# Dilated q in residue order, row sums in two parts, and a static instruction order from measured durations, in an attention and soft-MoE kernel

## The chip, the cores and the metric

The kernel runs on one core of a Trainium2 chip. The metric is the device time of one execution in microseconds (us). Within a profile, times count from the start of the span; the reported time is 1.7 to 1.8 us longer than the span. A ratio is the mean time of one kernel's fast runs over the mean of the other's fast runs of the same rounds, so it is not quite the ratio of the medians quoted beside it.

The engines: PE does matmuls, PEld its weight loads, ACT evicts and exponentiates, DVE transposes and multiplies, POOL issues the loads, SP issues the stores. The 16 DMA engines move the data. The granted clock is the share of PE's full clock that the profile shows as let through. Labels such as L731 are lines of that kernel's kernel.py; L1 and L2 alone are the two layers of the experts.

## The reference

Sliding-window attention (8 batches, 8 heads, 576 tokens, head size 64) and then a soft mixture of experts over all 4608 tokens. Cut to what matters:

```python
mask_plain = (rel >= 0) & (rel < 32)                                  # heads 0..3
mask_dil = (rel >= 0) & (rel < 128) & (rel % 4 == 0)                  # heads 4..7
attn = softmax(where(mask, q @ k.T / 8, -1e9)); x = concat_heads(attn @ v)   # (4608, 512)

logits = x @ phi                                      # 8 experts x 4 slots = 32 columns
d = softmax(logits, over tokens)
slot_input = d.T @ x                                  # needs ALL tokens
slot_out[e] = relu(slot_input[e] @ w1[e]) @ w2[e]     # needs all of w1 and w2
out = softmax(logits, over slots) @ slot_out          # (4608, 512) f32, 9.44 MB
```

No output row exists before the attention of every token is done, and none before every expert's w2 has been used. The inputs are 28 MB of q, k, v and 34 MB of weights.

## The kernel before

Attention works in 16 halves, a plain and a dilated one for each batch. Each operation is registered with a guessed duration and a priority; a small list scheduler simulates the five engines and the DMA queue and fixes one static order for each engine. On the chip each engine then runs its list strictly in order, waiting on semaphores. A wrong guess does no harm to the result; it can only put an operation at a bad place in a list.

```python
PE_SLOW = 1.5
LAT = 0.07                          # from the end of an op to where others see it
def pet(n, cols): return n * max(cols / 2.4, 30.0) * PE_SLOW / 1000.0
...
if o.kind == "dma":                 # the scheduler's model of a load
    qfree = max(qfree, o.end + 1.3) + o.bytes / 422e3
    o.vis = qfree + 1.5
```

q, k and v are turned by DVE in 32x32 blocks so that the head dimension lies on the partitions. In the dilated half a query block is every fourth token. A token's bf16 pair takes 4 bytes, so a step of four tokens is 8 elements, 16 bytes:

```python
dve.transpose(au(o_dst, [[1, 18], [18, 32]]), au(o_stg + ..., [[32, 18], [1, 32]]))   # q, k and v
...
pe.matmul(pf(h, 128 * rr, [[1, 128]]),                  # L477: 4 heads run side by side
          a(ok + 2 * res + par, [[8, 128]], 32 * h, 32),   # k: weights, 16-byte step
          a(oq + 2 * res + par, [[8, 128]], 32 * h, 32))   # q: moving, 16-byte step
pe.matmul(pf(h, 256, [[1, 64]]),                        # L484: the 64 left-over queries
          a(ok + 2 * (320 + 128 * r) + par, [[2, 128]], 32 * h, 32),
          a(oq + 1024 + par, [[2, 64]], 32 * h, 32))
```

The first layer (L1) and the transposes of its result are followed by 36 row-sum matmuls and the second layer (L2). L2 is cut into column halves s = 0 and 1, and into expert groups; the w2 of experts 6 and 7 is loaded last, as four column-half "slabs". So the first half of the columns can be finished, multiplied out and stored while the second-half slabs are still on their way. NA = 3 row groups of 512 rows are stored in halves, the other six whole.

```python
wq += [w2_slab(6, 0), w2_slab(7, 0), w2_slab(6, 1), w2_slab(7, 1)]      # the last loads
...
for es_ in ((0, 1, 2, 3), (4, 5), (6, 7)):
    for s in range(2):
        l2(es_, s)                                  # "L260" = experts 6,7, half 0; "L261" half 1
...
for G in range(NA):                                 # 12 first-half output tiles
    for j in range(4): out_tile(G, j, 0, 256, ...)  # PE matmul, then ACT or DVE evicts
    store(G, 0, 256, ...)
```

The softmax here doesn't subtract the row's maximum and nothing guards it: scores larger than these inputs give would overflow.

## Time and profile before

| | before |
|---|---|
| time, median of 4 | 186.97 us (186.74 to 187.33) |
| span | 185.3 us |
| last slot-input sum (end of attention) starts on PE | 140.2 us |
| L2 | 150.5 to 156.95 us |
| first store issued | 158.3 us |
| from the first store to the end of the span | 27 us |

The page's rows by 40 slices of 4.63 us, for the kernel before: a digit is the busy share in tenths, PEclk the granted clock, GB/s what the DMA engines wrote (loads turn f32 into bf16 on the way, so 211 GB/s written is 422 GB/s read).

```profile
PEclk9999999999999999999999979999965799999755
DMA  5999999999999999999999999999999990599996
GB/s 69 203 211 209 210 211 211 211 210 212 211 210 211 211 210 211 210 211 211 209 211 211 211 211 217 213 213 213 217 211 200 198 160 12 183 348 398 425 416 274
```

The load stream never stops until about 152 us. Then DMA is almost idle for a slice and a half, and then it stores to the end.

Groups of instructions by line and shape, for the kernel before. The columns after the bar are total busy us, the mean ns of one, and the idle time before them with what ended it.

```profile
L450 DVE STREAM_TRANSPOSE ar<-ar 128x576 uint32<-128x576 uint32 x48 | 57.5, 1245 | 9.1 <-DMA ar<-in_v_dram 3.4 <-PE ps L521 2.9 <-PE ps L484 1.7
L477 PE MATMUL ps<-ar 32*128 32x128 bf16 x256 | 18.2, 413 | 0.0
L477 PEld LDWEIGHTS ps<-ar 32*128 32x128 bf16 x256 | 8.3, 146 | 7.0 <-issue 5.0
L484 PE MATMUL ps<-ar 32*128 32x64 bf16 x128 | 4.1, 200 | 0.0
```

The timeline of PE and the store queue in the tail, for the kernel before: start, length, engine, line, count, and in brackets the wait before it. L685 is the last slot-input sum, L731 is L1, L765 the row sums, L781 is L2, L812 the output tiles.

```profile
140.20 0.75 PE L685 MATMUL ps<-ar 96*128 96x32 bf16 x22 [0.65 <-ACT ar L673]
141.84 4.82 PE L731 MATMUL ps<-ar 128*32 128x512 bf16 x48 [0.90 <-DVE ar L719]
148.22 1.36 PE L765 MATMUL ps<-ar 128*128 128x1 bf16 x36
150.48 6.47 PE L781 MATMUL ps<-ar 128*32 128x256 bf16 x128 [0.36 <-DVE ar L754]
156.88 3.37 PE L812 MATMUL ps<-ar 128*128 128x256 bf16 x18
158.29 14.50 SPq L831 DMA_DIRECT2D out_dram<-ar  x12
```

All 128 L2 matmuls run through in one block, with no wait for a weight: the last slab had landed before L2 came to it. The output tiles of both halves come after all of L2.

### The profile page before, as it was taken

The numbers are of one execution on the slowest core, as the hardware profiler recorded it, in microseconds if no ns is written. First come the engines' busy times: TensorE is split into PE (matmuls) and PEld (weight loads), VectorE is DVE, ScalarE is ACT, GpSimd is POOL, SyncE is SP. The second block draws the span as 40 slices with busy tenths as digits, with TensorE's granted clock in tenths as the row PEclk, the third lists the DMA queues.
The fourth block names the chain that finished last, engine by engine and source line by source line (L and its number), as shares of the span: only waits on it lengthen the run. The fifth ranks groups of instructions, "written<-read, shape, count | busy, mean of one in ns | idle before, by whom it ended". The sixth has DMA issues, their size and how long they took to land.

```text
span 185.3 us, 5336 instructions
## 1 busy us (share of the span) xinstructions
PE 132.0 (71%) x2268; PEld 90.2 (49%) x2268; DVE 113.9 (61%) x186; ACT 105.2 (57%) x167; POOL 51.5 (28%) x97
## 2 busy tenths in 40 slices
PE   0027897788797988798898699888566989984000
PEld 0014555567566657467567476656434477321000
DVE  6897277688997968697498596433601010997000
ACT  0008467776869779479769846957541411995000
POOL 7679813413424332323850000270000000000000
PEclk9999999999999999999999979999965799999755
DMA  5999999999999999999999999999999990599996
GB/s 69 203 211 209 210 211 211 211 210 212 211 210 211 211 210 211 210 211 211 209 211 211 211 211 217 213 213 213 217 211 200 198 160 12 183 348 398 425 416 274
DMA packets 21735, 40.78 MB, mean 220 GB/s; under 512 B 2000, under 2 KB 9168, under 8 KB 20944
## 3 DMA queue, kind: packets, MB, share of 16 engines
q0 software_dynamic: 17152, 30.94, 90.3%
q1 hardware_dynamic: 4560, 9.50, 13.5%
q8 instruction: 18, 0.29, 0.6%
q14 instruction: 5, 0.04, 0.1%
HBM read 61.93 MB, written 9.44 MB: 385 GB/s over the span
## 4 chain that ended last, share of the span: by engine, by line
PE 41%; ACT 17%; DVE 16%; DMA 12%; issue 5%; ACTq 0%; DVEq 0%; POOLq 0%
DMA ar<-in_v_dram 12%; ACT ar L499 9%; PE ps L460 7%; PE ps L477 7%; PE ps L812 5%; DVE ar L450 4%; DVE ar L565 4%; PE ps L781 3%; PE ps L554 3%; PE ps L731 3%; ACT ar L527 3%; PE ps L521 2%; ACT ar L621 2%; PE ps L644 2%; PE ps L467 2%
## 5 line engine op out<-in xcount | busy, mean ns | idle before, releaser
L450 DVE STREAM_TRANSPOSE ar<-ar 128x576 uint32<-128x576 uint32 x48 | 57.5, 1245 | 9.1 <-DMA ar<-in_v_dram 3.4
L499 ACT ACTIVATE ar<-ps 128x1152 bf16<-128x1152 f32 (+1 forms) x32 | 37.9, 1185 | 26.9 <-PE ps L484 22.7
L460 PE MATMUL ps<-ar 128*128 128x320 bf16 (+1 forms) x128 | 24.4, 318 | 18.6 <-DVE ar L450 12.5
L565 DVE TENSOR_TENSOR ar<-ps,fs 96x768 bf16<-96x768 f32 (+1 forms) x32 | 26.3, 823 | 1.3
L527 ACT ACTIVATE ar<-ps 128x768 bf16<-128x768 bf16 x32 | 24.8, 829 | 3.0 <-PE ps L521 2.9
L460 PEld LDWEIGHTS ps<-ar 128*128 128x128 bf16 x128 | 11.2, 103 | 23.2 <-DVE ar L450 13.8
L521 PE MATMUL ps<-ar 128*128 128x128 bf16 x192 | 17.3, 234 | 2.9 <-ACT ar L652 1.8
L554 PE MATMUL ps<-ar 128*128 128x65 bf16 x320 | 15.3, 199 | 5.0 <-ACT ar L499 2.3
L477 PE MATMUL ps<-ar 32*128 32x128 bf16 x256 | 18.2, 413 | 0.0
L561 DVE RECIPROCAL fs<-ps 96x12 f32<-96x12 f32 (+1 forms) x32 | 6.3, 196 | 17.8 <-PE ps L554 17.6
L824 DVE TENSOR_SCALAR ar<-ps,fs 128x256 f32<-128x256 f32 (+1 forms) x24 | 12.8, 609 | 7.0 <-PE ps L812 7.0
L554 PEld LDWEIGHTS ps<-ar 128*128 128x128 bf16 x320 | 12.6, 101 | 7.7 <-ACT ar L499 3.2
L521 PEld LDWEIGHTS ps<-ar 128*128 128x128 bf16 x192 | 13.1, 120 | 4.4 <-PE ps L554 1.9
L327 POOL DMA_DIRECT2D ar<-in_k_dram x16 | 9.3, 581 | 18.5 <-DVE ar L450 12.8
L327 POOL DMA_DIRECT2D ar<-in_v_dram x16 | 8.8, 551 | 17.3 <-DVE ar L450 6.8
L344 POOL DMA_DIRECT2D ar<-in_moe_w_dram x12 | 6.4, 584 | 24.1 <-DVE fs L693 24.1
L821 ACT ACTIVATE ar<-ps,fs 128x256 f32<-128x256 f32 (+1 forms) x24 | 12.2, 584 | 0.1
L812 PE MATMUL ps<-ar 128*128 128x256 bf16 (+1 forms) x48 | 11.2, 333 | 1.3 <-DVE ar L824 0.6
L337 POOL DMA_DIRECT2D ar<-in_moe_w_dram x16 | 11.7, 737 | 0.0
L477 PEld LDWEIGHTS ps<-ar 32*128 32x128 bf16 x256 | 8.3, 146 | 7.0 <-issue 5.0
L327 POOL DMA_DIRECT2D ar<-in_q_dram x16 | 8.8, 548 | 9.7 <-DVE ar L450 4.9
L644 PE MATMUL ps<-ar 128*128 128x288 bf16 x64 | 10.2, 307 | 1.2 <-ACT ar L628 1.2
(64 smaller groups left out, 163.1 us busy)
## 6 DMA issues: line engine op xcount, KB each, us to landing
ar<-in_moe_w_dram POOLq DMA_DIRECT2D x32, 512.0 KB, 24.9
out_dram<-ar SPq DMA_DIRECT2D x6, 1024.0 KB, 10.3
ar<-in_k_dram POOLq DMA_DIRECT2D x16, 288.0 KB, 20.4
ar<-in_q_dram POOLq DMA_DIRECT2D x16, 288.0 KB, 20.7
ar<-in_v_dram POOLq DMA_DIRECT2D x16, 288.0 KB, 20.4
out_dram<-ar SPq DMA_DIRECT2D x6, 512.0 KB, 6.3
fs<-in_moe_phi_dram SPq DMA_DIRECT2D x1, 64.0 KB, 1.9
```

The costliest lines, as they stand in the source:

```text
L327: return pool.dma_start(a(o_stg + (s * 3 + j) * 1152, [[1, 1152]]), src[b, 4 * dl:4 * dl + 4].rearrange("h (p t) d -> (h p) (t d)", p=32))
L450: op(DVE, lambda j=j, o_dst=o_dst: dve.transpose(au(o_dst, [[1, 18], [18, 32]]), au(o_stg + (st * 3 + j) * 1152, [[32, 18], [1, 32]])), 1. ...
L460: pe.matmul(pf(h, 0, [[1, W]]), a(o_id, [[1, 128]]), a(msk, [[1, W]]), start=True, stop=False)
L477: last = pe.matmul(pf(h, 128 * rr, [[1, 128]]), a(ok + 2 * res + par, [[8, 128]], 32 * h, 32), a(oq + 2 * res + par, [[8, 128]], 32 * h, 3 ...
L499: eo = op(ACT, lambda P=P, W=W: act.activation(a(P, [[W, 4], [1, W]]), AP(ps, 0, [[4096, 128], [512, 4], [1, W]]), ACTF.Exp, scale=SCALE), ...
L521: last = pe.transpose(pb(bank.idx, bb * 256 + par * 32, [[64, 4], [1, 32]]), src, a(o_id, [[1, 128]]))
L527: op(ACT, lambda t=t, bank=bank: act.activation(a(o_vb[vs] + 3 * t * VBK, [[66, 12], [2, 32], [1, 2]]), pb(bank.idx, 0, [[64, 12], [1, 32] ...
L554: last = pe.matmul(pf(bank.idx + x, 65 * t, [[1, 65]]), w, a(VB + t * VBK + 66 * h, [[1, 65]]), start=True, stop=True)
L565: op(DVE, lambda hp=hp, bank=bank: dve.tensor_tensor(a(ox + 128 * hp, [[64, 2], [256, NT], [1, 64]], 0, rows), pf(bank.idx, 0, [[512, 2], ...
L644: last = pe.matmul(pf(bank.idx, 0, [[1, 288]]), a(o_phis + 128 * c, [[1, 128]]), a(o_xt[xt] + 576 * c + 288 * g, [[1, 288]]), start=(c == ...
L812: op(PE, lambda: pe.matmul(pf(bank.idx, 0, [[1, cw]]), a(o_et + 512 * G + j, [[4, 128]]), a(o_so + c0, [[1, cw]]), start=True, stop=True), ...
L824: op(DVE, lambda: dve.tensor_scalar(dst, src(), sca, None, op0=AluOp.mult), dvet(cw, True), prio + .1, reads=[bank, b_rinv], writes=wr, na ...
```

## The change

Its intent: read dilated q with a 4-byte step, take most row sums out of the tail, and feed the scheduler durations and latencies measured for each kind of operation. Cut to its core:

```diff
-PE_SLOW = 1.5
+PE_SLOW = 1.1
-    LAT = 0.07
+    LAT = {"PE": 0.24, "ACT": 0.06, "DVE": 0.05, "POOL": 0.06, "SP": 0.06}
-        return n * max(cols / 2.4, 30.0) * PE_SLOW / 1000.0
+        return (40.0 + n * max(cols / 2.4, 27.0)) * PE_SLOW / 1000.0
...     (and new durations in about ten op() calls; the op that turns v on PE now
         also waits for the buffer it is evicted to, a part that no run isolates)
+            for x in range(4):       # dilated q only; else one transpose as before
+                na = (18 - x + 3) // 4
+                t0, t1 = x, 18 + x
+                at = [(t % 4) * 144 + t // 4 for t in (t0, t1)]
+                last = dve.transpose(
+                    au(o_dst + 2 * at[0], [[1, na], [9, 16], [at[1] - at[0], 2]]),
+                    au(src + 64 * x, [[128, na], [1, 32]]))
-                                a(oq + 2 * res + par, [[8, 128]], 32 * h, 32),
+                                a(oq + 288 * res + par, [[2, 128]], 32 * h, 32),
-                            a(oq + 1024 + par, [[2, 64]], 32 * h, 32),
+                            a(oq + 256 + par, [[2, 16], [288, 4]], 32 * h, 32),
...
+        if i == 13:
+            row_sums(0, 7, 15 * PERIOD)      # 28 of the 36 matmuls, inside attention
+    row_sums(7, 9, T1 + 4)                   # the other 8
-    op(PE, rs_fn, pet(36, 30), T1 + 3, ...)  # all 36, between L1 and L2
```

More of the change, by code (lines that the diff above doesn't have):

```diff
@@ L172, in run @@
             free[o.eng] = o.end
-            o.vis = o.end + self.LAT
+            o.vis = o.end + self.LAT[o.eng]
             if o.kind == "dma":
@@ L447, in half, with turn @@
         oq, ok = ok, oq
-        for j, o_dst in ((1, ok), (0, oq), (2, ov)):
-            op(DVE, lambda j=j, o_dst=o_dst: dve.transpose(
-                au(o_dst, [[1, 18], [18, 32]]),
-                au(o_stg + (st * 3 + j) * 1152, [[32, 18], [1, 32]])),
-               1.24, pr("T") + (0.5 if j == 2 else 0.0), reads=[b_stg[st][j]],
-               writes=[b_kqv[kq][j]], name=f"T{i}{'qkv'[j]}")
+        def turn(j, o_dst):
+            src = o_stg + (st * 3 + j) * 1152
+            if not (dl and j == 0):
+                return dve.transpose(au(o_dst, [[1, 18], [18, 32]]), au(src, [[32, 18], [1, 32]]))
+            for x in range(4):
[5 more added lines that the diff above has]
+                    au(src + 64 * x, [[128, na], [1, 32]]))
+            return last
+        for j, o_dst in ((1, ok), (0, oq), (2, ov)):
+            op(DVE, lambda j=j, o_dst=o_dst: turn(j, o_dst),
+               1.43 if dl and j == 0 else 1.24, pr("T") + (0.5 if j == 2 else 0.0),
+               reads=[b_stg[st][j]], writes=[b_kqv[kq][j]], name=f"T{i}{'qkv'[j]}")
         def sc_fn(r):
@@ L494, in half @@
             dr = 1.6 * r
-            op(PE, lambda r=r: sc_fn(r), 0.35 + pet(4, 300) + pet(6, 100), pr("SC") + dr,
+            op(PE, lambda r=r: sc_fn(r), (1.2 if dl else 0.9) * PE_SLOW, pr("SC") + dr,
                reads=[bq, bk, b_id, b_md if dl else b_mp],
@@ L523, in tb_fn @@
                 return last
-            op(PE, tb_fn, pet(6, 128), pr("TB") + 1.0 * t, reads=[bv, b_id], writes=[bank],
+            op(PE, tb_fn, pet(6, 128), pr("TB") + 1.0 * t, reads=[bv, b_id], writes=[bank, b_vb[vs][t]],
                name=f"TB{i}{t}")
@@ L557, in pv_fn @@
                 return last
-            op(PE, pv_fn, pet(2 * NT, 80), pr("PV") + 0.5 * hp, reads=b_vb[vs] + bP, writes=[bank],
+            op(PE, pv_fn, pet(2 * NT, 65), pr("PV") + 0.5 * hp, reads=b_vb[vs] + bP, writes=[bank],
                name=f"PV{i}{hp}")
@@ L582, in pz_fn @@
                 return last
-            op(PE, pz_fn, pet(8, 80), pr("PV") + 1.2, reads=b_vb[vs] + bP, writes=[bank],
+            op(PE, pz_fn, pet(8, 65), pr("PV") + 1.2, reads=b_vb[vs] + bP, writes=[bank],
                name=f"PZ{i}")
@@ L616, in half @@
             n = 6 if not dl else (2 if x else 8)
-            op(PE, xt_fn, pet(n, 110), pr("XT") + 0.4 * x, reads=[bx, b_id], writes=[bank],
+            op(PE, xt_fn, pet(n, 128 if dl else 96), pr("XT") + 0.4 * x, reads=[bx, b_id], writes=[bank],
                name=f"XT{i}{x}")
@@ L671, in half @@
         ek = b % 2
-        op(PE, et_fn, pet(11, 80), pr("ET"), reads=[b_et, b_sel], writes=[bank], name=f"ET{b}")
+        op(PE, et_fn, pet(11, 32), pr("ET"), reads=[b_et, b_sel], writes=[bank], name=f"ET{b}")
         op(ACT, lambda bank=bank: act.activation(
@@ L689, in si_fn @@
             return last
-        op(PE, si_fn, pet(22, 80), pr("SI"), reads=[b_ek[ek], b_xp[xi], b_xd[xi]], writes=[bank],
+        op(PE, si_fn, pet(22, 32), pr("SI"), reads=[b_ek[ek], b_xp[xi], b_xd[xi]], writes=[bank],
            name=f"SI{b}")
@@ L695, in half, with row_sums, fn @@
            dvet(128, True), pr("SA"), reads=[bank], rmw=[b_siacc], name=f"SA{b}")
+    def row_sums(g0, g1, prio):
+        bank = Bank(f"rs{g0}")
+        def fn():
+            last = None
+            for t in range(4 * g0, 4 * g1):
+                last = pe.matmul(pf(bank.idx, t, [[1, 1]]), a(o_et + 512 * (t // 4) + t % 4, [[4, 128]]),
+                                 a(o_rm, [[1, 1]]), start=True, stop=True)
+            return last
+        op(PE, fn, pet(4 * (g1 - g0), 72), prio, reads=[b_et, b_rm], writes=[bank], name=f"RS{g0}")
+        op(DVE, lambda: dve.reciprocal(f(o_rinv + 4 * g0, [[1, 4 * (g1 - g0)]]),
+                                       pf(bank.idx, 4 * g0, [[1, 4 * (g1 - g0)]])),
+           .2, prio + .2, reads=[bank], writes=[b_rinv], name=f"RR{g0}")
     last_ex = [None]
@@ L735, in l1_fn @@
                 return last
-            op(PE, l1_fn, pet(4, 560), T1 + 0.2 + g, reads=[b_sit] + b_w1[4 * g:4 * g + 4],
+            op(PE, l1_fn, pet(4, 900), T1 + 0.2 + g, reads=[b_sit] + b_w1[4 * g:4 * g + 4],
                writes=[bank], name=f"L1{g}{x}")
@@ L757, in bass_dilated_sliding_attn__then__soft_moe_slots_kernel @@
            reads=[bank], writes=[b_htz], name=f"HE{g}")
-    bank = Bank("rs")
-    def rs_fn(bank=bank):
-        last = None
-        for t in range(36):
-            last = pe.matmul(pf(bank.idx, t, [[1, 1]]), a(o_et + 512 * (t // 4) + t % 4, [[4, 128]]),
-                             a(o_rm, [[1, 1]]), start=True, stop=True)
-        return last
-    op(PE, rs_fn, pet(36, 30), T1 + 3, reads=[b_et, b_rm, b_sit], writes=[bank], name="RS")
-    op(DVE, lambda bank=bank: dve.reciprocal(f(o_rinv, [[1, 36]]), pf(bank.idx, 0, [[1, 36]])),
-       .2, T1 + 3.2, reads=[bank], writes=[b_rinv], name="RSr")
     sobank = [Bank("soA"), Bank("soB")]
@@ L785, in fn @@
             return last
-        op(PE, fn, pet(8, 270), T1 + 5 + 2 * es[0] + 20 * s,
+        op(PE, fn, pet(8, 300), T1 + 5 + 2 * es[0] + 20 * s,
            reads=[b_htz] + [b_w2[e][s] for e in es], rmw=[sobank[s]], name=f"L2{es[0]}{s}")
```

## The prediction

> **What bounds the kernel now.**
> 1. Loads: in the 40-slice view DMA is at 9 and moves about 211 GB/s (as written) from 5 us to 148 us; the slice at 153 to 157 us shows 12. So all inputs and weights are in at about 152 us, whatever the engines do.
> 2. Attention is slower than its inputs. In the timeline the same PE piece (a batch's first dilated scores, L460 then L477) stands at 62.2 and 77.2 us: 15.0 us a batch, PE busy 6.1 of every 7 us. A batch's loads with two weight pieces take about 13.3 us (estimate: 5.6 MB read at 2 x 211 GB/s). The last k, q, v land by about 111 us (estimate), but the last scores end at 127.1 and the last slot-input sum at 141.3.
> 3. The tail: L1 from 141.8 (clock granted 0.57), row sums L765 148.2 to 149.6, L2 150.5 to 156.9, first store issued at 158.3. From there to the end is 27 us, of which 9.44 MB at 425 GB/s is 22.
>
> So every us by which the first store comes earlier is a us of time, until the landing of the last weights sets it.
>
> **What the change does.**
> - *q in residue order.* In the dilated scores each group of four heads' matmuls (128 columns) takes (1.14 - 0.41)/3 = 0.24 us; in the plain ones (96 columns, step 4 bytes) (0.44 - 0.20)/5 = 0.05. The Trainium skill ("SBUF — State Buffer", cachelines note) says that accesses crossing a 16-byte line pay a penalty; q's step there is 16 bytes, so the trace agrees. With step 4 a group should take 0.1 (k, still 16 bytes, loads its weights in 141 ns, not 92). The 64 left-over queries get an inner step of 576 bytes: their two groups go from 0.05 to about 0.13. Net about 0.55 us per scores operation, 16 of them: 9 us of PE, nearly all on the critical path.
> - *Four transposes.* 1.245 us becomes about 1.43[...]: +1.5 us on DVE in all, which has room.
> - *Row sums.* 28 of 36 move into attention; 1.36 us between L1 and L2 becomes about 0.3: 1 us.
> - *Order.* Better costs should remove some waits of PE on ACT (5 us at L460 for L499), and let first-half outputs go before second-half L2. Worth 0 to 4 us; can go wrong.
>
> **Sum.** A batch falls from 15.0 to about 13.8 us, near the loads' 13.3. The last slot-input sum comes 8 to 10 us earlier, L2 could start at about 140. Then weights bound it: the first-half slabs of the last two experts land at about 147, first store at about 150, the second half lands at 152. About 8 of the 9 to 11 us gained reach the end. 152 + 22 + about 3 = 177 us span, plus 1.7 us between span and time: **179.5 us**. Range 176.5 to 184. Chances: faster by over 2% 0.86, within 2% 0.12, slower 0.02.
>
> **What would show it.** L477 x16 falls from 1.14 us to about 0.5, MATMUL mean from 413 ns to about 210; L484 rises. Batch period 13.5 to 14. Slot-input sum at 130 to 135. L2's last operations wait for the weight DMA. No slice near 12 GB/s between loads and stores.
>
> **What would make it wrong.** k's strided weight load bounds L477 (gain halved: about 183); the new order stalls PE or puts second-half L2 ahead of first-half outputs (first store at 154: 183); PE idles for loads and is granted less clock in the tail; stores slow the last loads.

## The result, and the profile after

| | before | after | predicted |
|---|---|---|---|
| time, median of 4 | 186.97 us | 184.78 us (183.87 to 184.89) | 179.5 (176.5 to 184) |
| ratio of fast runs | | 0.987 (0.9835 to 0.9906) | 0.96 |
| last slot-input sum starts | 140.2 | 132.5 | 130 to 135 |
| first-half slabs landed, L2 on them starts | (not waited for) | 149.8 | 147 |
| last slab landed | 154.1 | 155.2 | 152 |
| last L2 ends | 156.95 | 157.1 | not given |
| first store issued | 158.3 | 153.0 | 150 |
| span | 185.3 | 183.1 | 177 |

Attention did end 7.7 us earlier, inside the predicted window. The time fell by 2.2 us. The same three rows of the page, for the kernel after:

```profile
PEclk9999996999999999999999999995559995799755
DMA  5999999999999999999999999999999997299997
GB/s 69 201 211 207 211 210 213 211 210 214 208 212 212 208 210 213 209 209 211 211 213 209 212 209 217 212 217 212 214 215 207 197 192 159 71 341 397 408 428 317
```

The load stream looks as it did. The hole in DMA after it has moved by one slice and is narrower, but it is still there (71 GB/s). The groups that answer to those shown of before, for the kernel after:

```profile
L489 PE MATMUL ps<-ar 32*128 32x128 bf16 x256 | 7.8, 239 | 0.0
L489 PEld LDWEIGHTS ps<-ar 32*128 32x128 bf16 x256 | 5.5, 146 | 4.5 <-issue 4.5
L496 PE MATMUL ps<-ar 32*128 32x64 bf16 x128 | 6.3, 274 | 0.0
L458 DVE STREAM_TRANSPOSE ar<-ar 128x160 uint32<-128x160 uint32 x16 | 5.9, 442 | 0.4 <-DMA ar<-in_q_dram 0.4
L458 DVE STREAM_TRANSPOSE ar<-ar 128x128 uint32<-128x128 uint32 x16 | 4.8, 373 | 0.0
```

The dilated matmul fell from 413 to 239 ns, the weight load of k stayed at 146 ns, and the left-over matmul rose from 200 to 274 ns, all as predicted. The tail of the kernel after, on PE and the store queue (L697 is the last slot-input sum, L798 is L2, L829 the output tiles):

```profile
132.50 0.77 PE L697 MATMUL ps<-ar 96*128 96x32 bf16 x22 [0.31 <-ACT ar L685]
142.50 3.67 PE L798 MATMUL ps<-ar 128*32 128x256 bf16 x96 [0.84 <-DVE ar L785]
149.84 1.05 PE L798 MATMUL ps<-ar 128*32 128x256 bf16 x16 [3.67 <-DMA ar<-in_moe_w_dram]
151.37 1.47 PE L829 MATMUL ps<-ar 128*128 128x256 bf16 x6 [0.48 <-ACT ar L811]
155.21 1.89 PE L798 MATMUL ps<-ar 128*32 128x256 bf16 x16 [2.38 <-DMA ar<-in_moe_w_dram]
157.04 2.31 PE L829 MATMUL ps<-ar 128*128 128x256 bf16 x13
152.96 18.24 SPq L848 DMA_DIRECT2D out_dram<-ar  x12
```

This is the whole story in seven lines. L2 of experts 0 to 5 is done at 146.2 and then PE waits 3.7 us for the first-half slabs. Six of the twelve first-half output tiles follow. The list of PE then says "last L2", whose slab lands at 155.2, and the other six tiles, which need nothing more, stand behind it. Only one store is out by then; the second is issued at 158.25, where the first of before was issued at 158.29. And the last L2 takes 1.89 us where the same 16 matmuls took 1.05 at 149.84.

Two-us stretches of the kernel after, with busy us (and count) of each engine and, at the end of a row, the granted clock, DMA share and GB/s:

```profile
core 0: us, PE busy (x) PEld busy (x) DVE busy (x) ACT busy (x) POOL busy (x), PEclk, DMA share, GB/s
153.00:155.00 2.00, 0.00 (x0) 0.00 (x0) 0.36 (x1) 0.14 (x1) 0.00 (x0) 0.50 0.55 148
155.00:157.00 2.00, 1.79 (x16) 1.03 (x16) 0.00 (x0) 0.00 (x0) 0.00 (x0) 0.50 0.42 142
157.00:159.00 2.00, 1.98 (x14) 1.28 (x12) 1.31 (x4) 1.85 (x5) 0.00 (x0) 0.72 0.00 0
```

From 157 to 159 us DMA moves nothing. PE stood idle from 153 to 155 us, and the clock granted to it is 0.50 when the last L2 comes. The Trainium skill ("TensorE: Matmul & The Clock Gate", Part 1) names half clock as the throttled state, and here the 1.89 us against 1.05 us agree. It also says that an idle window of about 3.4 us brings half clock back, and this the trace of after does not bear out. The 16 matmuls right behind a wait of 3.67 us (at 149.84) ran in 1.05 us. The clock fell at 151.3 us, before the wait of 2.38 us began. And it was 0.50 from 124.0 to 137.7 us too (the 5s in the PEclk row), though no wait of PE in the 14 us before was longer than 1.4 us. What makes the clock fall stays open here.

### The profile page after: what moved, and what is told of

The parts are those of the page before. It is cut to its first block, busy times and chain, and to the rows that moved or that the text cites. A ratio compares the mean times of both kernels' runs of the same rounds, so it can differ in the third digit from the quotient of the medians.

```text
span 183.1 us, 5337 instructions
## 1 busy us (share of the span) xinstructions
PE 122.1 (67%) x2268; PEld 86.1 (47%) x2268; DVE 113.5 (62%) x211; ACT 105.3 (58%) x167; POOL 51.5 (28%) x97
## 3 DMA queue, kind: packets, MB, share of 16 engines
q1 hardware_dynamic: 4560, 9.50, 13.7%
## 4 chain that ended last, share of the span: by engine, by line
DMA 49%; DVE 20%; PE 14%; ACT 3%; issue 3%; POOL 2%; POOLq 0%; DVEq 0%; ACTq 0%
DMA ar<-in_moe_w_dram 21%; DMA ar<-in_k_dram 15%; DMA ar<-in_v_dram 14%; DVE ar L452 8%; PE ps L829 3%; DVE ar L577 3%; PE ps L472 3%; DVE ar L841 3%; ACT ar L511 3%; PE ps L566 2%; DVE ar L412 2%; PE ps L533 1%; PE ps L479 1%; DVE ar L417 1%; PE ps L798 1%
## 5 line engine op out<-in xcount | busy, mean ns | idle before, releaser
L452 DVE STREAM_TRANSPOSE ar<-ar 128x576 uint32<-128x576 uint32 x40 | 48.6, 1245 | 6.7 <-DMA ar<-in_k_dram 6.3
L472 PE MATMUL ps<-ar 128*128 128x320 bf16 (+1 forms) x128 | 23.8, 312 | 16.1 <-DVE ar L452 12.5
L539 ACT ACTIVATE ar<-ps 128x768 bf16<-128x768 bf16 x32 | 25.7, 826 | 3.6 <-PE ps L533 3.6
L327 POOL DMA_DIRECT2D ar<-in_v_dram x16 | 8.8, 550 | 13.8 <-DVE ar L452 8.4
L636 ACT ACTIVATE ar<-ps 128x1024 bf16<-128x1024 bf16 x8 | 8.2, 1022 | 7.6 <-PE ps L623 7.6
L829 PE MATMUL ps<-ar 128*128 128x256 bf16 (+1 forms) x48 | 11.5, 362 | 1.4 <-ACT ar L811 0.5
L798 PE MATMUL ps<-ar 128*32 128x256 bf16 x128 | 6.6, 291 | 6.9 <-DMA ar<-in_moe_w_dram 6.0
## 6 DMA issues: line engine op xcount, KB each, us to landing
ar<-in_moe_w_dram POOLq DMA_DIRECT2D x32, 512.0 KB, 27.9
```

The lines of the kernel that those rows point to most:

```text
L327: return pool.dma_start(a(o_stg + (s * 3 + j) * 1152, [[1, 1152]]), src[b, 4 * dl:4 * dl + 4].rearrange("h (p t) d -> (h p) (t d)", p=32))
L452: return dve.transpose(au(o_dst, [[1, 18], [18, 32]]), au(src, [[32, 18], [1, 32]]))
L472: pe.matmul(pf(h, 0, [[1, W]]), a(o_id, [[1, 128]]), a(msk, [[1, W]]), start=True, stop=False)
L539: op(ACT, lambda t=t, bank=bank: act.activation(a(o_vb[vs] + 3 * t * VBK, [[66, 12], [2, 32], [1, 2]]), pb(bank.idx, 0, [[64, 12], [1, 32] ...
L829: op(PE, lambda: pe.matmul(pf(bank.idx, 0, [[1, cw]]), a(o_et + 512 * G + j, [[4, 128]]), a(o_so + c0, [[1, cw]]), start=True, stop=True), ...
```

## The experiments

The theory after reading the two traces (called A): *from about 150 us on, the time is set by when the weight slabs land and by what stands before and behind the last L2 on PE. Attention that ends earlier only waits longer.* Its rivals: the static order made attention faster and q did nothing (B); the time follows attention one for one (C); early stores don't help, or only slow the loads (D).

Twelve kernels ran, four to a chip, with five rounds each. The medians of before on the three chips were 186.7, 187.3 and 187.5 us, so the ratios are the better numbers.

### q alone, in the kernel before

The turn, its four transposes and the two new steps were put into before. No duration was touched, and the order of all engines was confirmed to be that of before.

```diff
+        def turn(j, o_dst): ...                # as in the change
-                a(oq + 2 * res + par, [[8, 128]], 32 * h, 32),
+                a(oq + 288 * res + par, [[2, 128]], 32 * h, 32),
-                a(oq + 1024 + par, [[2, 64]], 32 * h, 32),
+                a(oq + 256 + par, [[2, 16], [288, 4]], 32 * h, 32),
```

> The kernel before with the turned q and its four transposes alone; the instruction order is that of before. Theory A (the end is set by the landing of the last weight slabs at 154 to 155 us; work on PE before that is hidden beyond some 2 us): attention ends 6 to 9 us earlier (last slot-input sum at 132 to 135, not 141.3), but the last L2 waits for the slab and ends at about 155.5, first store at about 157; time 185 to 186. Rival B (the gain of the change comes from its instruction order, q brings little even inside attention): last slot-input sum at 138 or later, time 186.5 to 187. Rival C (time follows attention one for one): 179 to 181.

186.43 us, ratio 0.9983 (0.9956 to 1.0009): nothing that can be told from before. Rival C is out. Between A and B this run does not decide: the last slot-input sum started at 137.4 us, 2.8 us earlier than in before and not the 6 to 9 that A expected, and the time lies just above A's range and just below B's. DVE now waited for the inputs instead:

```profile
DVE ar L452 <- DMA ar<-in_v_dram: 6.4, 4, 4.0
DVE ar L452 <- DMA ar<-in_k_dram: 2.9, 4, 0.9
```

These are two rows of the waits of q_only (total us, times, longest); before has one such row, of 3.4 us. Part of the freed PE time became waiting for q, k, v. The 2.8 us that did arrive at the tail were spent in front of the slab: the first store came at 157.7, 0.6 us earlier than in before.

### Everything but q

```diff
-            if not (dl and j == 0):
+            if True:                           # one transpose, natural order
-                a(oq + 288 * res + par, [[2, 128]], 32 * h, 32),
+                a(oq + 2 * res + par, [[8, 128]], 32 * h, 32),
-                a(oq + 256 + par, [[2, 16], [288, 4]], 32 * h, 32),
+                a(oq + 1024 + par, [[2, 64]], 32 * h, 32),
```

> The kernel after with q in its natural order again (16-byte step, one transpose); instruction order and row sums as in after. Theory A: attention ends 4 to 8 us later than in after (slot-input sum at 137 to 141, not 133.3); L2 then ends at 155 to 157, near the slab's landing, so only 0 to 2 us of that reach the time: 185 to 187. Rival B: below 185.5 and attention nearly as early as in after. Rival C: 190 or more.

184.30 us, ratio 0.9873 (0.9841 to 0.9904), the same as the whole change (0.987). It was slightly faster than theory A expected. So of the change's 1.3%, order and row sums bring all. In this profile they bring it with attention as late as in before (the last slot-input sum started at 140.0 us), which speaks against rival B; but a later run with the same attention program shows 135.9, so how much the order does for attention is not settled. That the time does not come from there is what the next two runs test.

### The last L2 before all first-half tiles

If the gain lies in the place of the last L2, taking that place away must take the gain away, and leave attention as fast as it is.

```diff
+    by = {o.name: o for o in sc.ops}
+    for G in range(3):
+        for j in range(4):
+            by[f"O{G}{j}0"].ord = by["L261"]   # an edge for the scheduler, no semaphore
```

> The kernel after (turned q, split row sums, its order) with one edge: the last second-half L2 stands before all first-half output tiles, as in before. Attention still ends near 133 us. Theory A (what the time gained came from first-half outputs going out before the last slab is worked off, not from attention): first store at 157.5 to 158.5, time 186 to 187, all of the change's gain gone though attention is 8 us earlier. Rival C (attention's gain reaches the time): 184.3 to 185.2, as after.

187.51 us, ratio 1.0014 (0.999 to 1.0038), 0.5 us above the expected range. The whole gain is gone, though the last slot-input sum started at 134.25 us, 6 us earlier than in before. L2 and the first store of l2_first:

```profile
150.31 1.05 PE L798 MATMUL ps<-ar 128*32 128x256 bf16 x16 [2.41 <-DMA ar<-in_moe_w_dram]
155.46 1.89 PE L798 MATMUL ps<-ar 128*32 128x256 bf16 x16 [4.09 <-DMA ar<-in_moe_w_dram]
158.96 6.60 SPq L848 DMA_DIRECT2D out_dram<-ar  x6
```

6 us of earlier attention have become 2.4 us and 4.1 us of waiting for slabs, and a last L2 at half clock. Rival C is refuted.

### Only the place of the last L2, in the kernel before

The mirror image: the old q, the old row sums, the old durations, and two edges.

```diff
+    by["L260"].ord = by["L241"]       # experts 0..5 of both halves first
+    by["L261"].ord = by["O230"]       # all 12 first-half tiles before the last L2
```

> The kernel before with two ordering edges in the tail alone: the last experts' L2 after the other experts' L2, and all first-half output tiles before the last second-half L2. No change to attention, q or row sums. Theory A: first store at about 156.5, no idle DMA after it, time 184 to 185: as fast as the whole change. Rival C: attention still ends at 141, so 186.5 or more.

185.26 us, ratio 0.9887 (0.9858 to 0.9917), just above the expected range: two edges give what the whole change gives (0.987), with the last slot-input sum at 141.0 us. Its tail, by PE and the store queue:

```profile
150.60 4.64 PE L781 MATMUL ps<-ar 128*32 128x256 bf16 x112 [0.32 <-DVE ar L754]
157.13 8.22 SPq L831 DMA_DIRECT2D out_dram<-ar  x7
157.78 1.05 PE L781 MATMUL ps<-ar 128*32 128x256 bf16 x16
```

The last L2 starts 2.6 us later than in after and the time is about the same, because the first-half stores run meanwhile.

### All twelve tiles before the last L2, in the kernel after

```diff
+    by["L261"].ord = by[f"O{NA - 1}30"]
```

> The kernel after with one ordering edge: all twelve first-half output tiles stand before the last experts' second-half L2 on PE, not six. Theory A: the six tiles no longer wait behind the slab landing at 155.2; three first-half stores go out by about 155 and fill the 4 us in which DMA is idle (156 to 160): time 182 to 183, 2 to 2.5 us less than after. Rival D (the store phase starts when the second half is there, whatever came before; early stores only delay the slabs): slabs land 1 us or more later and the time stays at 184.5 to 185.

182.68 us, ratio 0.9786 (0.9755 to 0.9818), which is 0.8% under after's ratio. Rival D is refuted: the last slab had landed at 155.1 us and was used at 155.27, within 0.1 us of after. The tail of outs_first, and its stretches:

```profile
151.71 2.11 PE L829 MATMUL ps<-ar 128*128 128x256 bf16 x12 [0.57 <-ACT ar L811]
155.27 1.05 PE L798 MATMUL ps<-ar 128*32 128x256 bf16 x16 [1.45 <-DMA ar<-in_moe_w_dram]
```

```profile
155.00:157.00 2.00, 1.21 (x17) 0.94 (x18) 0.00 (x0) 0.38 (x1) 0.00 (x0) 0.90 1.02 343
157.00:159.00 2.00, 2.00 (x11) 1.44 (x10) 1.53 (x4) 1.74 (x5) 0.00 (x0) 0.50 0.98 328
```

DMA is busy from 155 to 159 us, where after had 142 GB/s and then none. PE's wait is 1.45 us and not 2.38, and the last L2 runs at full clock (1.05 us).

Why did the scheduler put only six tiles there? Its own simulation answers it. Printed from the order it built for after (simulated end of issue, when the data is seen):

```
w2s_70   seen at 146.29 us     the chip: first-half L2 waits until 149.84
w2s_71   seen at 151.26 us     the chip: 155.2
L261     simulated start 151.26, after tile O110, the sixth
```

The change corrected the durations of the engines and left the model of the loads 3.5 to 4 us early. In the simulation the last slab is there when the sixth tile is done. On the chip it is not, and an in-order engine can't step around it.

### outs_first without q

> outs_first with q in its natural order. Attention ends at about 140.8, L2 of the first half at about 153.8 and not 151.1, so the first store at about 155.6 and not 153.0. Theory A says that what q gains in attention (7.5 us) can reach the time only as far as the first-half slabs' landing at 150 lets it: here up to 2.7 us earlier first store; time 183 to 184.3, 0.5 to 1.5 us over outs_first. If q is worth nothing even then: 182.7 as outs_first.

The edit is that of "everything but q" on top of the edge. 183.19 us, ratio 0.9775 (0.9742 to 0.9807): no slower than outs_first (0.9786). The expected 0.5 to 1.5 us did not appear. In this profile attention's last sum started at 135.9 us, 4 us earlier than in no_q, which has the same attention program, and not at the expected 140.8. The first-half slabs had landed by 148.7 us, and L2 ran through with no wait for them:

```profile
145.16 4.58 PE L798 MATMUL ps<-ar 128*32 128x256 bf16 x112 [0.57 <-PE ps L780]
```

So the case that the expectation was about, L2 late because of attention, did not occur in it. One profile each is a poor measure of the end of attention (see below); the six times of each are not. After against no_q (0.987 and 0.9873) and outs_first against no_q_outs (0.9786 and 0.9775, on two chips) say the same: q in residue order is worth nothing measurable with either tail.

### Whole rows instead of slabs

```diff
-    for e in range(6):
+    for e in range(8):
         wq += [w2_piece(e, 0), w2_piece(e, 4)]
-    wq += [w2_slab(6, 0), w2_slab(7, 0), w2_slab(6, 1), w2_slab(7, 1)]
```

> The kernel after with the last two experts' w2 loaded in whole-row pieces (8 KB runs) instead of column-half slabs (1 KB runs). If the slabs' short runs are why the last weights land at 155.2 and not at the 152 of the prediction: last landing at 152 to 153 us and no slow slices from 142 to 154. If the drain of the queue is why: still 154 to 155. Without the halves the first store comes after both L2, at landing plus about 3.5 us; time 183 to 185.5.

187.91 us, ratio 1.0047 (1.0007 to 1.0086): slower than before, and 2.4 us above the expected range. It was to show whether the short runs of the slabs make the landing late. They don't: L2 waited for the last weights until 155.0 us here too.

```profile
155.00 3.44 PE L797 MATMUL ps<-ar 128*32 128x256 bf16 x32 [5.59 <-DMA ar<-in_moe_w_dram]
```

But the rate did hold up longer, and then tapered off: 209 GB/s at 149 to 150 us, then 147, 98, 45, 16, 8. So the lateness is in the drain of the queue, and the halves are worth keeping: without them the first store came at 159.8 us. One impurity: with the halves gone, all of L2 stands before all the tiles, as in l2_first. The intervals of the two ratios (1.0047 and 1.0014) overlap, so this run shows no loss beyond that of the early tiles.

The trace holds for each load the 16 moments at which the DMA engines reported their part done. The distance from the first to the last of the 16:

```
                         after    before
a load near 50 us        2.0      1.9  us
a load near 110 us       3.1      3.0
the last slab            4.25     3.1
```

The reports move apart in steps. In after, the weight loads landing from 26 to 79 us show 2.0 us, those from 87 to 146 us 3.1, and the last three 4.2: at each step one or two of the 16 reports come about 1.1 us later and stay so. The mean rate says that the bytes are in by 152 us; the slowest engine is 2 to 3 us behind. The Trainium skill states the rule in "DMA: Bandwidth & Descriptors", section "Why a DMA increments its semaphore by 16 and not by 1": the engines finish independently, and only the full 16 means that all data has landed. The records agree. Why the engines fall back stays open. The last step is not tied to the change: the last slab shows 4.1 us in q_only and 4.8 in before_tail, which are built on before.

### Less to load

The direct test of what bounds each kernel: leave out expert 7's w2 (2.1 MB read) and use expert 6's in its place. The result is wrong. The order of every compute engine was confirmed to be unchanged (in the kernel after, with an edge that holds the last L2 behind the sixth tile).

```diff
-    wq += [w2_slab(6, 0), w2_slab(7, 0), w2_slab(6, 1), w2_slab(7, 1)]
+    wq += [w2_slab(6, 0), w2_slab(6, 1)]
-    a(w2off(e) + DM * c + 256 * s, [[1, 256]])
+    a(w2off(min(e, 6)) + DM * c + 256 * s, [[1, 256]])
```

> The kernel before without the load of the last expert's w2 (2.1 MB less read; that expert uses the weights of the one before it, so the result is wrong on purpose); all engines' order unchanged. Loads end about 5 us earlier. Theory A: in before the last L2 already ends 2 to 3 us after its slab has landed, so time follows PE, not the loads: 186 to 187.3, within 0.5% of before. If the loads bound before too: 182.

> The kernel after with the same 2.1 MB left out (wrong result on purpose), order of all engines unchanged. Theory A: the last slab lands at about 150 and not 155.2; L2 has been waiting for it, so the second-half L2 ends at about 152.5 and not 157.1: time 180 to 181.5, 3.5 to 4.5 us less than after. If the wait for slabs is not what holds after: 184 or more.

Before: 187.33 us, ratio 1.0003 (0.9978 to 1.0028). 5 us less of loading is worth nothing there. After: ratio 0.9537 (0.9498 to 0.9575) from its two fast runs, 178.33 and 178.95 us; its other four runs, 181.04 to 182.41 us at a clock of 0.868 to 0.880, count as slow. The fast runs are 6 us under after, more than the 3.5 to 4.5 expected. How much is not firm: other kernels have fast runs at a clock of 0.873, and all six runs together give a ratio of 0.964, about 4 us under after. Either way it is clear of noise. So the change moved the bound: in before the tail waits for PE, in after PE waits for the weights.

### Row sums back in one block

```diff
-        if i == 13:
-            row_sums(0, 7, 15 * PERIOD)
-    row_sums(7, 9, T1 + 4)
+    row_sums(0, 9, T1 + 3)            # after L1, as in before
```

> The kernel after with the 36 row-sum matmuls back in one block before the second transposed-hidden operation. The prediction put 1 us on this. Theory A: L2 of the first experts starts 1 us later, but PE has 3 to 4 us of waiting for the first-half slabs there: 184.3 to 185.2, as after. If row sums are on the path: 185.8.

185.41 us, ratio 0.9899 (0.9867 to 0.9932), between the two expectations. Against after's 0.987 the intervals overlap. The first L2 started at 144.3 us, and the L2 on the first-half slabs at 150.05 after a wait of 2.1 us, where after has 149.84: the 1.35 us block disappeared in that wait. One impurity: the scheduler left four tiles and not six before the last L2 here.

### Starting the stores earlier

If the stores are to fill the drain of the loads, the first half has to be complete earlier. Expert 5 was loaded in halves too, all first halves ahead of all second halves, and more row groups were stored in halves.

```diff
-    for e in range(6):
+    for e in range(5):
         wq += [w2_piece(e, 0), w2_piece(e, 4)]
-    wq += [w2_slab(6, 0), w2_slab(7, 0), w2_slab(6, 1), w2_slab(7, 1)]
+    wq += [w2_slab(e, s) for s in range(2) for e in (5, 6, 7)]
-    for es_ in ((0, 1, 2, 3), (4, 5), (6, 7)):
+    for es_ in ((0, 1, 2, 3), (4,), (5, 6, 7)):
-    NA = 3
+    NA = 5                            # early5; early4 has 4
+    by["L251"].ord = by[f"O{NA - 1}30"]
```

> outs_first with the halves widened: expert 5's w2 in column halves too, order of loads 5,6,7 first halves, then 5,6,7 second halves, five and not three row groups stored in halves. First-half slabs land at about 147.5 and not 150, first store at about 150.5, while the load queue still drains (150 to 154); last slab lands at 155 to 156.5. If the drain of the loads can be filled with stores: time 181 to 182. If early stores only slow the loads: 182.7 or more.

> early5 with four and not five row groups stored in halves: 0.5 us less of DMA at the lower rate of 1 KB runs (345 against 420 GB/s), but up to 1 us of idle DMA before the second halves. 181.3 to 182.5, level with early5.

early5: 181.98 us, ratio 0.9716 (0.9691 to 0.9741), the best, correct, and 1.6% under after by the ratios (0.9716/0.987), so it beats both kernels. early4: 182.97 us, ratio 0.9764 (0.9728 to 0.9799). In early5 DMA moves 315 GB/s or more in every microsecond from 153 to 166 us, where after had its hole. early4 runs out of first halves: its profile shows 61 and 20 GB/s at 159 to 161 us, with its last L2 at half clock again (1.89 us). By the ratios the fifth group, which theory called level, is worth 0.5%, but the two intervals still touch.

## Why the prediction was right or wrong

**What bounds before: right.** Loads at 211 GB/s, attention slower than its inputs, an idle DMA before the stores. fewer_before shows that weights don't bound it.

**The cost of q: right as PE time.** A group of four heads fell from 0.24 us to (0.48 - 0.24)/3 = 0.08; from the first dilated to the last left-over matmul a scores operation fell from 1.20 to 0.70 us, 8 us over 16 of them (the prediction: 9). The Trainium skill's note on cachelines ("SBUF — State Buffer", the part on the DMA port swizzle) agrees, in both directions: the 4-byte step got faster, the 576-byte one slower.

**"Nearly all on the critical path": wrong.** q alone moved the end of attention by 2.8 us and the time by 0.3, which can't be told from nothing. Where the whole change shortened attention, the batch period fell from (91.55 - 62.17)/2 = 14.7 us to (100.91 - 59.70)/3 = 13.7 us (predicted 13.8). These are the first dilated scores of a batch, two batches apart in before and three in after:

```profile
62.17 0.70 PE L460 MATMUL ps<-ar 128*128 128x320 bf16 x4
91.55 0.70 PE L460 MATMUL ps<-ar 128*128 128x320 bf16 x4 [0.57 <-ACT ar L499]
```

```profile
59.70 0.70 PE L472 MATMUL ps<-ar 128*128 128x320 bf16 x4
100.91 0.72 PE L472 MATMUL ps<-ar 128*128 128x320 bf16 x4
```

The sum was right and its parts were not, so it is partly luck that the end of attention fell into the predicted window: q and order work together, and against the arrival of the inputs. In profiles of kernels with after's order, q and full loads the last slot-input sum starts anywhere from 132.5 to 135.6 us, so a few us of this are not settled by single profiles.

**The transposes: off, without effect.** Four take 1.17 to 1.22 us together on DVE, not 1.43, because they overlap (their durations add up to 1.63); one took 1.25.

**The row sums: right in size, wrong in place.** 1.36 us did leave the path between L1 and L2. That path had 3.7 us of waiting at its end, and rows_back shows no clear loss.

**The failing step: "About 8 of the 9 to 11 us gained reach the end".** It rested on slabs landing at 147 and 152 us, which came from the mean rate. They land at 149.8 and 155.2 because a load is complete when the slowest of 16 DMA engines is, and at the last slab their reports are 4.25 us apart. Here is the largest term that was mis-sized, 3 us. That the last slab of before had landed at 154.1 could have been read from the times from issue to landing beforehand. The premise in front of that step failed as well, that every us by which the first store comes earlier is a us of time: in after it came 5.3 us earlier than in before and the time fell by 2.2, in before_tail it came only 1.2 us earlier, and the ratio is the same within the noise (0.9887 against 0.987). In after the first store stood alone until 158.25.

**Two named risks came true.** "Puts second-half L2 ahead of first-half outputs" happened for six of twelve tiles; outs_first puts it at 0.8%, about 1.6 us. "PE idles for loads and is granted less clock in the tail" happened: 0.84 us on the last L2. They may not be added to the 1.6, for the last L2 of outs_first ran in 1.05 us. The profiles add up: outs_first ended 25.1 us after the landing of its last slab, as the prediction's 22 + 3 had it, and after 27.9 us after. So of the 6 us between the predicted span (177) and the measured one (183.1), 3.2 are the landing and 2.9 what stood behind it, of which outs_first's 1.6 us is the share that all runs confirm. The prediction had given them too little weight: it called the order's worth "0 to 4 us" on top, when the order of the tail was all that the change gained in time (l2_first and before_tail).

## What to carry to other kernels

Before adding up savings on a busy engine, find the next event that its results must wait for, and when it really happens: a load is there when its last DMA engine reports, not when the mean rate says so. Where engines run fixed lists, look at each wait for data and at what stands behind it in the same list; two ordering edges there were worth as much as the whole change here. And when a schedule comes from a model, correct the model of the transfers together with that of the engines, or the better half will trust the worse one.

## What the Trainium skill lacked or had wrong

- "SBUF — State Buffer", the note on cachelines: its closing figure (free up to 8 bf16) can be read as allowing a step of 8. A step of 8 bf16 elements for the moving operand cost 0.24 us for 128 columns with four heads side by side, a step of 2 cost 0.08. The mechanism stated there (two hits on a line) fits; the figure does not. The page has no number for the matmul's penalty.
- "DMA: Bandwidth & Descriptors": it says that the 16 engines finish independently and that two of them are usually slower, but not how far apart the reports of one load can be at the end of a long stream. Here the spread grew in steps from 2.0 us near 50 us to 4.25 us at the end, and set when the last weights were usable. Which engines were late the records don't say.
- "DMA: Bandwidth & Descriptors", table of specifications: it asks for at least 512 bytes for line rate. Stores in runs of 1 KB moved 342 GB/s (160 to 166 us of after), those of whole rows 423 GB/s (168 to 180 us). No run here isolates the run length as the cause.
- "TensorE: Matmul & The Clock Gate", Part 1: half clock is as stated (1.89 us against 1.05 us for the same 16 matmuls), but its condition, an idle window of about 3.4 us, is not what this shows: half clock from 124.0 to 137.7 us in after with no wait of PE over 1.4 us in the 14 us before, and full clock right behind a wait of 3.67 us.
